# Block attention with routed experts on one core: the four expert slots of under 256 tokens, from fp32 matmuls to three products of split operands

## The chip, the cores and the metric

The kernel runs on one core of a Trainium2 chip. The metric is the device time of one execution in microseconds (us); of before there are three runs. PE is TensorE, DVE VectorE, ACT ScalarE, POOL GpSimd, and SP is the engine that issues most transfers. A profile's span runs from the first to the last instruction of one profiled execution.

## The reference

Two parts are computed. First, attention over 8 batches, 8 heads, 576 positions of 64 values, masked by blocks of 64 positions:

```python
mask = block_i >= block_j
scores = np.where(mask, scale * np.matmul(q, k.transpose(0, 1, 3, 2)), -1e9)
attn = softmax(scores)
x = np.matmul(attn, v)        # as 4608 tokens of 512 values
```

Then each token picks a group and, in it, an expert (16 experts in all, by two argmaxes), and goes through that expert's two layers:

```python
h = np.maximum(xg[mask_e] @ w1[g, e], 0.0)    # 512 -> 1024
ye = h @ w2[g, e]                             # 1024 -> 512
out[tok_idx] = combined[:, None] * ye
```

All inputs and the output are fp32.

## The kernel before

The kernel has an attention stage, and behind it an expert stage, which is the one that the change touches. Attention of 32 pairs of heads is laid out by a list of steps, with the routing of finished batches woven in. In the routing, tokens are counted by expert, and a table of token numbers is written to DRAM.

**Slots.** The expert stage works through slots. A slot is one expert with a fixed room for `T` tokens. One early slot, "e", has 512. Then come 14 slots in the order of `EXEC` (line 423), with `T = 16 * CAPS`: 528, 144, 448, 144, 448, 192, 416, 256, 320, 256, 320, 288, 272 and 128. Four of them have under 256 tokens: 144, 144, 192 and 128. Before the change they carry `small=True` (line 866).

**Weights.** Each expert's weights are eight units of 512 KB: units 0, 2, 4 and 6 are column blocks of w1, units 1, 3, 5 and 7 are row blocks of w2. A unit is loaded by SP into one of four `raw` buffers (`load`, line 915). Then two pieces of 512 columns are made of it (`piece`, line 922). ACT casts the piece to the type fp32r, as the high part `wh` (line 936), and DVE subtracts that from the fp32 piece and writes the remainder as the low part `wl` (line 937). A small slot's w1 units are handled otherwise: SP loads them straight into a `wh` buffer as fp32 (line 928), with no cast and no `wl`. There are 9 buffers each for `wh` and `wl`.

**Tokens.** `xt` (line 943) transposes gathered rows on PE into PSUM (line 953). ACT copies the high part `xh` out (line 960), and DVE makes the low part `xl` (line 961). For a small slot ACT makes one fp32 copy (line 958), and there is no `xl`.

**The first layer,** `g1` (line 963), writes `h`. For each block of 128 hidden values and each of four parts of 128 inputs it does three fp32r matmuls, wh·xh, wh·xl and wl·xh (line 985). For a small slot it does one fp32 matmul in their place (line 980). Such a matmul has as many moving columns as the slot has tokens (half as many where that is 528). Each of them has its own weight load, which the profile lists apart, as PEld. Slots of 256 tokens or fewer handle several hidden blocks in one call: two blocks for 144, 192 and 256, four blocks for 128. So a slot of 144 or 192 tokens has four calls of g1, and the slot of 128 has two.

**The second layer,** `g2` (line 1016), multiplies split `h` by split w2 with 512 moving columns (lines 1030 and 1035). It is the same for all slots.

**Order.** PE's order is a fixed list, `seq` (line 1062): a g1 call, then the g2 call of the call of g1 before it. Behind each of these steps, `run` lets `advance` (line 1120) issue up to two pieces, by due times that `plan` works out from an assumed time on PE (line 1086): four passes over the columns for a small slot's g1, three for others. `pump` (line 1112) keeps up to four units in raw buffers ahead of the unit that is being split.

Of the kernel before, what the change touches and what calls it, by code (L numbers as in the profile page):

```python
# [17 lines left out]
P = 128  # L18
# [815 lines left out]
class Moe:  # L834
# [25 lines left out]
    def slot(self, n, m, row, idx):  # L860
        T = UNIT * m
        nf, r = divmod(T, P)
        ch = [(c, P) for c in range(nf)] + ([(nf, r)] if r else [])
        nk = 1 if T > 256 else min(8, 1 << (512 // T).bit_length() - 1)
        return dict(n=n, m=m, T=T, gap=32 if r <= 32 else 64, nf=nf + (r > 64), tail=r if r <= 64 else 0, ch=ch, row=row, idx=idx, u={}, x={},
                    small=T < 256, nk=nk, nb=8 // nk)

    def index(self, s):
        if "e" in s:
# [39 lines left out]
            src, n = self.w2[bass.ds(s["e"], 1), z:z + 256, :], 2  # L909
        return src.rearrange("o (c p) f -> p (o c) f", p=P), n  # L910

    def direct(self, s, u):
        return s["small"] and u % 2 == 0

    def load(self, s, u):
        self.index(s)
        raw = self.raw.tile([P, 1024], F32, tag="raw", name=f"raw{s['n']}_{u}")
# [3 lines left out]

    def piece(self, s, u, z):
        nc = self.nc
        if self.direct(s, u):
            self.index(s)
            h = self.wh.tile([P, 1024], F32R, tag="wh", name=f"wh{s['n']}_{u}")
            src, n = self.wsrc(s, u)
            nc.sync.dma_start(h.bitcast(F32).rearrange("p (c f) -> p c f", c=n), src)
            s["u"][u] = (h,)
            return  # L930
        if z == 0:
            s["u"][u] = (self.wh.tile([P, 1024], F32R, tag="wh", name=f"wh{s['n']}_{u}"),
                         self.wl.tile([P, 1024], F32R, tag="wl", name=f"wl{s['n']}_{u}"))
        h, l = s["u"][u]
        sl = slice(z * 512, (z + 1) * 512)
        nc.scalar.copy(h[:, sl], s["raw", u][:, sl])  # L936
        nc.vector.tensor_tensor(out=l[:, sl], in0=s["raw", u][:, sl], in1=h[:, sl].bitcast(F32), op=ALU.subtract)  # L937
# [5 lines left out]
    def xt(self, s, c):  # L943
        nc = self.nc
        if "xt" not in s:
            s["xt"] = self.at.pt.tile([P, PTB], F32R, tag="pt", name=f"xt{s['n']}")
            s["xh"], s["xl"] = [s["xt"][:, PTB // 2 * z:PTB // 2 * z + 4 * s["T"]].rearrange("p (d w) -> p d w", d=4)
                                for z in range(2)]
        c, n = s["ch"][c]
        ps = self.at.psT(f"xp{s['n']}_{c}")  # L950
        pv = ps[:, 0:4 * n].rearrange("p (d w) -> p d w", d=4)
        for dc in range(4):
            nc.tensor.transpose(out=pv[:, dc, :], in_=s["x"][c][0:n, dc * P:(dc + 1) * P],  # L953
                                identity=self.c["ident"][0:n, 0:n])
        xh = s["xh"][:, :, c * P:c * P + n]
        xl = s["xl"][:, :, c * P:c * P + n]
        if s["small"]:
            nc.scalar.copy(xh.bitcast(F32), pv)
            return
        nc.scalar.copy(xh, pv)  # L960
        nc.vector.tensor_tensor(out=xl, in0=pv, in1=xh.bitcast(F32), op=ALU.subtract)

    def g1(self, s, b):
        nc = self.nc
        nk, T, r = s["nk"], s["T"], s["tail"]
        n = nk * T
        w0 = n if n <= 512 else n // 2
        ps = []
        for a in range(0, n, w0):
            p = self.at.ps_s.tile([P, 1, 512], F32, tag="S", name=f"h{s['n']}_{b}_{a}")[:, 0, 0:w0]  # L970
            ps.append((a, p))
            tw = min(T, w0)
            for k in range(w0 // tw):
                kg = b * nk + k
                w = self.w(s, 2 * (kg // 2))
                f = slice(kg % 2 * P, kg % 2 * P + P)
                o, t = p[:, k * tw:(k + 1) * tw], slice(a, a + tw)
                for dc in range(4):
                    if s["small"]:
                        nc.tensor.matmul(o, lhsT=w[0][:, dc, f].bitcast(F32), rhs=s["xh"][:, dc, t].bitcast(F32),  # L980
                                         start=dc == 0, stop=dc == 3)
                        continue
                    wh, wl = w
                    for x, (ww, rr) in enumerate(((wh, s["xh"]), (wh, s["xl"]), (wl, s["xh"]))):
                        nc.tensor.matmul(o, lhsT=ww[:, dc, f], rhs=rr[:, dc, t],  # L985
                                         start=dc == 0 and x == 0, stop=dc == 3 and x == 2)
        buf = self.hbuf()
        F = T - r
        pad = s["gap"] - r if r else 0
        L = T + pad  # L990
        g = buf[:, 0:nk * (L + T)].rearrange("p (k t) -> p k t", k=nk)
        hi, lt, lf = g[:, :, 0:T], g[:, :, L:L + r], g[:, :, L + r:L + T]
        if pad:
            nc.gpsimd.memset(g[:, :, T:L].bitcast(F32), 0.0)
        for a, p in ps:
            wa = min(T, w0)
            pv = p.rearrange("p (k t) -> p k t", t=wa)
            nc.scalar.activation(hi[:, :, a:a + wa], pv, AF.Relu)  # L998
            for t, t0, t1 in ((lf, 0, F), (lt, F, T)):
                q0, q1 = max(a, t0), min(a + wa, t1)  # L1000
                if q0 < q1:
                    nc.vector.scalar_tensor_tensor(out=t[:, :, q0 - t0:q1 - t0], in0=pv[:, :, q0 - a:q1 - a], scalar=0.0,  # L1002
                                                   in1=hi[:, :, q0:q1].bitcast(F32), op0=ALU.max, op1=ALU.subtract)
        s["h", b] = (hi, lf, g[:, :, F:L + r])
# [56 lines left out]
    def plan(self, slots):  # L1061
        self.slots = slots
        seq = []
        prev = None
        for o, s in enumerate(slots):
            s["o"] = o
            s["wide"] = o % 2 == 0
            for b in range(s["nb"]):
                seq.append((s, "g1", b))
                if b == 0:  # L1070
                    if prev is not None:
                        seq.append(prev)
                else:
                    seq.append((s, "g2", b - 1))
            prev = (s, "g2", s["nb"] - 1)
        seq.append(prev)
        self.seq = seq
        self.units = [(s, u) for s in slots for u in range(8)]
        self.first, self.last = {}, {}
        self.tc0, t = [], 0.0  # L1080
        self.begin = {}
        for n, (s, f, b) in enumerate(seq):
            self.tc0.append(t)
            nk = s["nk"]
            if f == "g1":
                t += nk * 4 * s["T"] * (4 if s["small"] else 3) / 2.4
            else:
                t += nk * (3 * s["nf"] + 2 * (s["tail"] > 0)) * 216
            if (f, b) == ("g1", 0):
                self.begin[s["o"]] = n  # L1090
                t += 430.0 * len(s["ch"])
            for k in range(b * nk, (b + 1) * nk):
                key = (s["o"], 2 * (k // 2) + (f == "g2"))
                self.first.setdefault(key, n)
                self.last[key] = n
        self.tc0.append(t)
        self.pieces = []
        for ui, (s, u) in enumerate(self.units):
            for z in range(1 if self.direct(s, u) else 2):
                self.pieces.append((ui, s, u, z))  # L1100
        self.due = [0.0] * len(self.pieces)
        nxt = 1e18
        for p in range(len(self.pieces) - 1, -1, -1):
            ui, s, u, z = self.pieces[p]
            nxt = min(self.tc0[self.first[s["o"], u]] - LEAD, nxt - PIECE)
            self.due[p] = nxt
        self.lq = [(s, u) for s, u in self.units if not self.direct(s, u)]
        self.nload = self.ndone = self.pos = 0
        self.gq = [(s, c) for s in slots for c in range(len(s["ch"]))]
        self.ngat = self.nxt = 0  # L1110
# [9 lines left out]
    def advance(self, k, limit, ready=False):  # L1120
        while k > 0 and self.pos < len(self.pieces):
            ui, s, u, z = self.pieces[self.pos]
            if ui > limit or (s["o"] > 0 and not ready):
                return
            if not self.direct(s, u) and ("raw", u) not in s:
                self.pump(ready)
            self.piece(s, u, z)
            self.pos += 1
            k -= 1
            if z == 1:  # L1130
                self.ndone += 1
            self.pump(ready)
# [50 lines left out]
    def overflow(self, cnti, row):  # L1183
        nc = self.nc
        hi = nc.values_load(cnti[0:1, 0:1], min_val=0, max_val=R - 1)
        with self.tc.For_i(0, hi, 1) as iv:
# [1 line left out]
            s["wide"] = False  # L1188
            self.gather(s, 0)
            for u in range(8):  # L1190
                if not self.direct(s, u):
                    self.load(s, u)
                for z in range(1 if self.direct(s, u) else 2):
                    self.piece(s, u, z)
            self.xt(s, 0)
            for b in range(s["nb"]):
# [123 lines left out]
```

## Time and profile before

| | us |
|---|---|
| three runs, median (lowest to highest) | 886.28 (885.41 to 886.73) |
| the profiled execution | 885.69 |
| its span | 883.6 |
| its mean granted clock, as a share of full | 0.994 |

The profile has a page, with busy time by engine and the chain of work that ended last, and views of its trace: groups of instructions, waits, a timeline, and busy time by stretch. In the timeline, neighbouring instructions of one kind are merged into one row. Its second number runs from the start of the first to the end of the last. PE's matmuls overlap, so a row's length is the spacing of its matmuls plus the full length of the last one.

### The profile page before, as it was taken

The numbers are of one execution on the slowest core, as the hardware profiler recorded it, in microseconds if no ns is written. First come the engines' busy times: TensorE is split into PE (matmuls) and PEld (weight loads), VectorE is DVE, ScalarE is ACT, GpSimd is POOL, SyncE is SP. The second block draws the span as 40 slices with busy tenths as digits, with TensorE's granted clock in tenths as the row PEclk, the third lists the DMA queues.
The fourth block names the chain that finished last, engine by engine and source line by source line (L and its number), as shares of the span: only waits on it lengthen the run. The fifth ranks groups of instructions, "written<-read, shape, count | busy, mean of one in ns | idle before, by whom it ended". The sixth has DMA issues, their size and how long they took to land.

```text
span 883.6 us, 17134 instructions
## 1 busy us (share of the span) xinstructions
PE 851.7 (96%) x5649; PEld 712.1 (81%) x5649; DVE 571.7 (65%) x1390; ACT 523.2 (59%) x1374; POOL 245.4 (28%) x469
## 2 busy tenths in 40 slices
PE   6889999999999999998989999999999999999996
PEld 4767878888887878776768878888888888988885
DVE  6657888889897979867824254365354655556562
ACT  5878888888897978774324244243343544545451
POOL 6443231424232232432523122122112121122011
PEclk9999999999999999999999999999999999999999
DMA  6988987878887877663245473474565566565471
GB/s 134 213 206 204 229 190 174 192 162 186 175 188 163 185 176 173 142 204 122 61 163 157 138 239 122 144 232 143 162 207 167 162 218 220 188 199 194 155 241 38
DMA packets 194041, 153.91 MB, mean 174 GB/s; under 512 B 126854, under 2 KB 158086, under 8 KB 193952
## 3 DMA queue, kind: packets, MB, share of 16 engines
q1 hardware_dynamic: 184704, 128.17, 55.9%
q0 software_dynamic: 9248, 24.64, 7.9%
q8 instruction: 46, 0.75, 0.3%
q14 instruction: 43, 0.35, 0.1%
HBM read 100.88 MB, written 24.59 MB: 142 GB/s over the span
## 4 chain that ended last, share of the span: by engine, by line
PE 88%; DMA 6%; DVE 3%; issue 2%; ACT 1%; SPq 0%; POOLq 0%; POOL 0%; DVEq 0%; ACTq 0%
PE y L1030 18%; PE h L985 18%; PE o L329 10%; PE tp L297 10%; PE s L254 9%; PE y L1035 4%; PE h L980 3%; DMA qk<-qk 3%; PE tp L176 3%; PE s L263 3%; PE xn L681 2%; PE xp L953 2%; PE lg L699 2%; PE ye L1030 2%; PE he L985 1%
## 5 line engine op out<-in xcount | busy, mean ns | idle before, releaser
L278 ACT ACTIVATE pb<-s,nm 128x384 f32<-128x384 f32 (+4 forms) x288 | 158.2, 560 | 28.3 <-DVE nm L268 25.3
L268 DVE TENSOR_REDUCE nm<-s 128x1 f32<-128x384 f32 (+4 forms) x288 | 141.4, 516 | 42.2 <-PE s L254 35.1
L985 PE MATMUL h<-xt,wh 128*128 128x264 f32 (+6 forms) x704 | 155.3, 312 | 0.0
L254 PE MATMUL s<-qk 128*128 128x384 f32 (+3 forms) x512 | 129.5, 351 | 11.9 <-DMA qk<-qk 5.5
L937 DVE TENSOR_TENSOR wl<-raw,wh 128x512 fp32r<-128x512 f32 x192 | 123.4, 684 | 10.6 <-ACT wh L936 10.3
L985 PEld LDWEIGHTS h<-xt,wh 128*128 128x128 f32 x704 | 119.3, 188 | 9.0
L309 ACT COPY pt<-tp 128x512 f32<-128x512 f32 (+1 forms) x224 | 113.2, 552 | 8.4 <-PE tp L297 5.4
L297 PE MATMUL tp<-ident,pb 128*128 128x128 f32 x800 | 117.2, 275 | 0.1
L985 PE MATMUL h<-xt,wl 128*128 128x264 f32 (+6 forms) x352 | 109.3, 311 | 0.0
L936 ACT CAST wh<-raw 128x512 fp32r<-128x512 f32 x192 | 109.1, 620 | 0.2
L1030 PE MATMUL y<-wh,hring 128*128 128x512 f32 x306 | 107.2, 401 | 0.0
L297 PEld LDWEIGHTS tp<-ident,pb 128*128 128x128 f32 x800 | 93.0, 141 | 13.6 <-DVE tmp L719 3.4
L329 PE MATMUL o<-pt,vb 128*64 128x320 f32 (+4 forms) x896 | 100.4, 362 | 2.3 <-ACT xT L309 1.3
L1002 DVE SCALAR_TENSOR_TENSOR hring<-h,hring 128x32 fp32r<-128x32 f32 (+7 forms) x112 | 35.7, 356 | 103.4 <-ACT hring L998 96.5
L998 ACT ACTIVATE hring<-h 128x288 fp32r<-128x288 f32 (+7 forms) x62 | 28.9, 467 | 118.3 <-PE h L985 53.7
L329 PEld LDWEIGHTS o<-pt,vb 128*64 128x64 f32 x896 | 60.0, 136 | 42.4 <-issue 3.5
L254 PEld LDWEIGHTS s<-qk 128*128 128x128 f32 x512 | 78.7, 190 | 19.2 <-ACT pb L278 9.9
L1056 POOL DMA_INDIRECT out_dram<-ys,ids x40 | 42.2, 1054 | 186.9 <-DVE ys L1052 157.3
L900 POOL DMA_INDIRECT xg<-xd,ids x40 | 41.7, 1043 | 103.7 <-DMA ids<-tab 48.7
L985 PEld LDWEIGHTS h<-xt,wl 128*128 128x128 f32 x352 | 66.2, 188 | 1.2
L1030 PEld LDWEIGHTS y<-wh,hring 128*128 128x128 f32 x306 | 57.6, 188 | 11.7
L1030 PE MATMUL y<-wl,hring 128*128 128x512 f32 x153 | 60.5, 395 | 0.0
(228 smaller groups left out, 1391.4 us busy)
## 6 DMA issues: line engine op xcount, KB each, us to landing
raw<-in_moe_w_dram SPq DMA_DIRECT2D x96, 512.0 KB
qk<-qk SPq DMA_DIRECT2D x93, 288.0 KB
natk<-in_k_dram SPq DMA_DIRECT2D x32, 256.0 KB
natq<-in_q_dram SPq DMA_DIRECT2D x32, 256.0 KB
vb<-in_v_dram SPq DMA_DIRECT2D x64, 128.0 KB
xd<-xns SPq DMA_DIRECT2D x32, 256.0 KB
wh<-in_moe_w_dram SPq DMA_DIRECT2D x16, 512.0 KB
tab<-fill POOLq DMA_DIRECT2D x10, 512.0 KB
```

What stands on the lines that cost most here:

```text
L254: nc.tensor.matmul(st[:, 0, 0:w], lhsT=r[a][z][:, q0:q0 + P], rhs=r[c][z][:, 0:w], start=x == 0, stop=x == 1)
L268: self.nc.vector.tensor_reduce(out=r["nm"][:, t:t + 1], in_=r["s", t], op=ALU.max, axis=AX.X if t < 8 else AX.XY, negate=True)
L278: nc.scalar.activation(reg, r.pop(("s", t)), AF.Exp, bias=r["nm"][:, t:t + 1], accum_out=self.sms[b][:, pr, t % 2, t // 2:t // 2 + 1])
L297: nc.tensor.transpose(out=o, in_=pb[:, POFF[x] + j * P:POFF[x] + (j + 1) * P], identity=self.c["ident"])
L309: self.nc.scalar.copy(dst, src)
L329: nc.tensor.matmul(o[64 * a:64 * a + 64, BLK * (t - b0):n], lhsT=r["v"][:, a, j, :], rhs=p[:, a], start=x == 0, stop=x == len(pcs) - 1, ti ...
L900: self.nc.gpsimd.indirect_dma_start(out=x[0:n], out_offset=None, in_=src, in_offset=bass.IndirectOffsetOnAxis(ap=s["ids"][0:n, c, 0:1], ax ...
L936: nc.scalar.copy(h[:, sl], s["raw", u][:, sl])
L937: nc.vector.tensor_tensor(out=l[:, sl], in0=s["raw", u][:, sl], in1=h[:, sl].bitcast(F32), op=ALU.subtract)
L985: nc.tensor.matmul(o, lhsT=ww[:, dc, f], rhs=rr[:, dc, t], start=dc == 0 and x == 0, stop=dc == 3 and x == 2)
L1030: nc.tensor.matmul(y[c][0:n], lhsT=hh, rhs=w, start=k == 0 and x == 0, stop=k == 7 and x == 2)
L1056: i = nc.gpsimd.indirect_dma_start(out=self.out, out_offset=bass.IndirectOffsetOnAxis(ap=s["ids"][0:n, c, 0:1], axis=0), in_=ys[0:n], in_o ...
```

## The change

The flag `small` goes, and with it each place that asked for it. The four small slots are treated as the others: their w1 units go through a raw buffer, the cast and the subtraction, their tokens get a low part, and g1 does three fp32r matmuls where it did one fp32 matmul. The planner counts three passes for them, and two pieces for each w1 unit where it counted one. The loop for overflowing tokens at the end, which has a slot of 128, changes likewise.

```diff
     def piece(self, s, u, z):
-        if self.direct(s, u):
-            self.index(s)
-            h = self.wh.tile([P, 1024], F32R, tag="wh", name=f"wh{s['n']}_{u}")
-            src, n = self.wsrc(s, u)
-            nc.sync.dma_start(h.bitcast(F32).rearrange("p (c f) -> p c f", c=n), src)
-            s["u"][u] = (h,)
-            return
...
         xl = s["xl"][:, :, c * P:c * P + n]
-        if s["small"]:
-            nc.scalar.copy(xh.bitcast(F32), pv)
-            return
         nc.scalar.copy(xh, pv)
         nc.vector.tensor_tensor(out=xl, in0=pv, in1=xh.bitcast(F32), op=ALU.subtract)
...
                 for dc in range(4):
-                    if s["small"]:
-                        nc.tensor.matmul(o, lhsT=w[0][:, dc, f].bitcast(F32), rhs=s["xh"][:, dc, t].bitcast(F32),
-                                         start=dc == 0, stop=dc == 3)
-                        continue
                     wh, wl = w
...
-                t += nk * 4 * s["T"] * (4 if s["small"] else 3) / 2.4
+                t += nk * 4 * s["T"] * 3 / 2.4
...
-            for z in range(1 if self.direct(s, u) else 2):
+            for z in range(2):
...
-        self.lq = [(s, u) for s, u in self.units if not self.direct(s, u)]
+        self.lq = list(self.units)
```

On PE, at the second g1 call of the first slot of 144 tokens (`h_1_0`; `y_4` and `y_0` are outputs of g2, `xt` holds the tokens), the order was:

```order
L1035 MATMUL y_4_6814<-wh_7_7071,hring 48x512
L1035 MATMUL y_4_6814<-wl_7_7072,hring 48x512
L980 MATMUL h_1_0_7281<-xt_7127,wh_2_7202 128x144 x8
L1030 MATMUL y_0_7300<-wh_1_7180,hring 128x512
L1030 MATMUL y_0_7300<-wl_1_7181,hring 128x512
```

and now begins as follows (the last two of these rows come eight times in all):

```order
L1013 MATMUL y_3_6813<-wh_7_7071,hring 128x512
L1018 MATMUL y_4_6814<-wh_7_7071,hring 48x512
L1018 MATMUL y_4_6814<-wl_7_7072,hring 48x512
L968 MATMUL h_1_0_7313<-xt_7133,wh_2_7196 128x144 x2
L968 MATMUL h_1_0_7313<-xt_7133,wl_2_7197 128x144
```

Eight matmuls in a call have become 24; their place among the others is the same.

On SP, where the loads of that slot's units stand (`raw_1` is unit 1 in a raw buffer, `wh_0` unit 0 loaded directly; the `raw` rows between two `wh` rows here are of the next slot), the order was:

```order
L919 DMA raw_7_7077<-in_moe_w_dram 128x2x512
L928 ISA
L928 DMA wh_0_7111<-in_moe_w_dram 128x4x256
L919 ISA
L919 DMA raw_0_7186<-in_moe_w_dram 128x4x256
L928 ISA
L928 DMA wh_2_7202<-in_moe_w_dram 128x4x256
L919 ISA
L919 DMA raw_1_7223<-in_moe_w_dram 128x2x512
```

and is now:

```order
L916 DMA raw_3_7077<-in_moe_w_dram 128x2x512
L916 ISA
L916 DMA raw_4_7117<-in_moe_w_dram 128x4x256
L916 ISA
L916 DMA raw_5_7194<-in_moe_w_dram 128x2x512
L916 ISA
L916 DMA raw_6_7216<-in_moe_w_dram 128x4x256
L916 ISA
L916 DMA raw_7_7253<-in_moe_w_dram 128x2x512
```

The eight units are loaded in the order in which PE uses them; before, unit 7 stood ahead of unit 0.

On ACT, in the slot of 272 tokens just ahead of the last slot (`hring` rows evacuate g1's output, `CAST` rows are pieces), the order was:

```order
L998 ACTIVATE hring<-h_3_0_10585 128x272
L936 CAST wh_6_10581<-raw_6_10456 128x512
L936 CAST wh_7_10614<-raw_7_10511 128x512
L998 ACTIVATE hring<-h_4_0_10618 128x272
L936 CAST wh_7_10614<-raw_7_10511 128x512
L936 CAST wh_1_10649<-raw_1_10536 128x512 x2
L998 ACTIVATE hx<-h_5_0_10655 128x272
```

and is now:

```order
L981 ACTIVATE hring<-h_3_0_10863 128x272
L926 CAST wh_7_10859<-raw_7_10781 128x512
L926 CAST wh_0_10884<-raw_0_10806 128x512 x2
L926 CAST wh_1_10900<-raw_1_10841 128x512
L981 ACTIVATE hring<-h_4_0_10904 128x272
L926 CAST wh_1_10900<-raw_1_10841 128x512
L926 CAST wh_2_10925<-raw_2_10857 128x512 x2
L926 CAST wh_3_10941<-raw_3_10882 128x512
L981 ACTIVATE hx<-h_5_0_10945 128x272
```

Between two evacuations there are now four casts, where there were two or three.

## Rows read from the trace of the kernel before

**Rows 1.** The page: busy us, share and instructions; the granted clock in 40 slices.
```profile
PE 851.7 (96%) x5649; PEld 712.1 (81%) x5649; DVE 571.7 (65%) x1390; ACT 523.2 (59%) x1374; POOL 245.4 (28%) x469
PEclk9999999999999999999999999999999999999999
```

**Rows 2.** Busy us by stretch, the expert stage: PE, PEld, DVE, ACT, POOL, clock, DMA share, GB/s.
```profile
500.00:876.00 376.00, 374.86 (x2097) 325.98 (x2095) 193.70 (x401) 161.73 (x315) 78.26 (x127) 1.00 0.57 181
```

**Rows 3.** PE's waits from 400 us on: us in total, times, longest.
```profile
PE xp L953 <- DMA xg<-xd,ids: 4.2, 1, 4.2
PE h L980 <- DMA wh<-in_moe_w_dram: 1.1, 1, 1.1
```

**Rows 4.** Chain of work that ended last, in order of time: start, us, what.
```profile
520.39 7.21 DMA wh<-in_moe_w_dram
...
573.60 1.96 PE h L980 x16
...
634.35 2.60 PE h L980 x16
...
695.87 2.86 PE h L985 x24
...
861.69 3.57 PE h L980 x32
```

**Rows 5.** Groups on PE from 500 us: shapes, count; busy us, mean ns of one.
```profile
L985 PE MATMUL h<-xt,wh 128*128 128x256 f32 x128 | 23.3, 282 | 0.0
...
L980 PE MATMUL h<-xt,wh 128*128 128x144 f32 x128 | 17.1, 287 | 1.1 <-DMA wh<-in_moe_w_dram 1.1
...
L980 PE MATMUL h<-xt,wh 128*128 128x192 f32 x64 | 11.2, 328 | 0.0
...
L980 PE MATMUL h<-xt,wh 128*128 128x128 f32 x64 | 7.5, 275 | 0.0
```

**Rows 6.** Timeline of weight loads (PEld): start, us, line, tile, shapes, count.
```profile
300.57 0.19 PEld L254 LDWEIGHTS s<-qk 128*128 128x128 f32 x1
350.98 0.30 PEld L254 LDWEIGHTS s<-qk 128*128 128x128 f32 x2
697.02 0.30 PEld L985 LDWEIGHTS h<-xt,wh 128*128 128x128 f32 x2
```

**Rows 7.** Timeline of PE, attention scores: two fp32r matmuls of 128 columns.
```profile
300.56 0.33 PE L254 MATMUL s<-qk 128*128 128x128 f32 x2
```

**Rows 8.** Timeline of weight loads and PE around another such pair.
```profile
304.08 0.30 PEld L254 LDWEIGHTS s<-qk 128*128 128x128 f32 x2
304.32 0.14 PEld L176 LDWEIGHTS tp<-ident,natq 128*128 128x128 f32 x1
...
304.10 0.42 PE L254 MATMUL s<-qk 128*128 128x128 f32 x2
304.36 0.41 PE L176 MATMUL tp<-ident,natq 128*128 128x128 f32 x2
```

**Rows 9.** Groups on ACT and DVE from 500 us: shapes, count; busy, mean ns.
```profile
L936 ACT CAST wh<-raw 128x512 fp32r<-128x512 f32 x176 | 100.0, 620 | 0.2
...
L937 DVE TENSOR_TENSOR wl<-raw,wh 128x512 fp32r<-128x512 f32 x176 | 113.1, 683 | 9.3 <-ACT wh L936 9.1
L961 DVE TENSOR_TENSOR xt<-xp,xt 128x512 fp32r<-128x512 f32 x21 | 14.4, 688 | 16.0 <-ACT xt L960 12.6 <-issue 3.2
```

**Rows 10.** Timeline of PE: starts of two g1 calls of the 272 slot.
```profile
844.26 0.41 PE L985 MATMUL h<-xt,wh 128*128 128x272 f32 x2
...
847.61 0.42 PE L985 MATMUL h<-xt,wh 128*128 128x272 f32 x2
```

**Rows 11.** Transfers from 500 us on: GB/s in 40 slices.
```profile
GB/s 161 203 332 72 169 187 171 123 289 141 159 140 181 114 253 276 83 240 110 179 109 248 175 233 244 189 183 228 101 291 179 121 236 182 136 204 232 176 55 30
```

More of the change, by code (lines that the diff above doesn't have):

```diff
@@ L865, in slot @@
         return dict(n=n, m=m, T=T, gap=32 if r <= 32 else 64, nf=nf + (r > 64), tail=r if r <= 64 else 0, ch=ch, row=row, idx=idx, u={}, x={},
-                    small=T < 256, nk=nk, nb=8 // nk)
+                    nk=nk, nb=8 // nk)
     def index(self, s):
@@ L910, in wsrc @@
         return src.rearrange("o (c p) f -> p (o c) f", p=P), n
-    def direct(self, s, u):
-        return s["small"] and u % 2 == 0
     def load(self, s, u):
@@ L1124, in advance @@
                 return
-            if not self.direct(s, u) and ("raw", u) not in s:
+            if ("raw", u) not in s:
                 self.pump(ready)
@@ L1190, in overflow @@
             for u in range(8):
-                if not self.direct(s, u):
-                    self.load(s, u)
-                for z in range(1 if self.direct(s, u) else 2):
+                self.load(s, u)
+                for z in range(2):
                     self.piece(s, u, z)
```

## The prediction

> **What bounds the kernel now.** I read the page first: PE is busy for 851.7 of 883.6 us, at the full granted clock in every slice [rows 1]. The change lies in the expert stage alone, so that stage comes next. From 500 to 876 us PE is busy for 374.86 of 376 us, DVE for 193.7, ACT for 161.7 and the transfers for 0.57 of their time [rows 2]. In such a stage a microsecond added on PE is a microsecond of the kernel, and ACT and DVE have room. PE's waits confirm it: past 500 us it waited once, 1.1 us, for a transfer into `wh`, the direct load of a small slot [rows 3]. That load took 7.21 us from issue to landing [rows 4]. The question is therefore what three fp32r matmuls take on PE where one fp32 matmul stood. A matmul's listed length does not tell it, since matmuls overlap; the spacing does.
>
> **What is removed.** A small slot has 8 hidden blocks times 4 input parts, 32 fp32 matmuls. The profile lists each as two records: 128 for the two slots of 144, 64 for that of 192 and 64 for that of 128 [rows 5], so each matmul goes through PE twice. The chain of work gives what the calls took, free of overlap [rows 4]: 1.96 us for 16 records of 144 columns, 2.60 us for 16 of 192 and 3.57 us for 32 of 128. That is 0.122, 0.162 and 0.112 us a record. With 8 calls of 144, 4 of 192 and 2 of 128, the calls take 8 × 1.96 + 4 × 2.60 + 2 × 3.57 = 33.2 us. The direct loads go too, and with them the 1.1 us wait.
>
> **What is added on PE.** Three fp32r matmuls for each fp32 one are 3 × 32 × 4 = 384 records in place of 256. What is one worth, at 128 to 192 columns? The expert stage has no fp32r matmul below 256 columns. There the call of 24 takes 2.86 us [rows 4], 0.119 each. This is the bound from above: fewer columns should not cost more.
>
> The bound from below is the weight load, as each matmul has its own. Two loads of 128 weight columns merged in a row last 0.30 us, where one lasts 0.19, so the second starts 0.11 us after the first, for attention's fp32r scores as for w1 [rows 6]. Across these rows that spacing does not shrink, neither for 256 columns nor for 128 [rows 8]. With rounding, it is at least 0.105 us. A matmul of 128 columns does not stream that long: in a pair of fp32r matmuls in the scores, the second starts 0.05 to 0.06 us after the first (0.33 us for both, less the 0.275 us that one of 128 lasts) [rows 5, 7]. So the stream gets short and the load stays: below 256 columns the load sets the pace, and columns that are saved give nothing back. The fp32 calls of 128 columns, whose load is of the same size, run at 0.112 us a record. This is the nearest row, and I take it, between 0.105 and 0.119.
>
> Per call, 24 × 0.112 = 2.68 us for 144 and 192 columns, and 48 × 0.112 = 5.36 us for 128. The differences are 0.72 × 8 = 5.8 us for the slots of 144, 0.08 × 4 = 0.3 us for that of 192, and 1.79 × 2 = 3.6 us for that of 128: together +9.7 us. The bounds: 384 × 0.105 − 33.2 = +7.1 us and 384 × 0.119 − 33.2 = +12.5 us. An fp32 matmul went through PE twice, each time for about two cycles a column (0.162 us × 2.4 GHz / 192); three fp32r passes at some 1.1 cycles a column (0.119 × 2.4 / 256) would be fewer cycles, but they need three weight loads instead of two, and that is what these short slots pay for.
>
> **What is added elsewhere.** 16 units of w1 are now split, in 32 pieces: 32 × 0.62 = 19.8 us on ACT and 32 × 0.683 = 21.9 us on DVE, and seven subtractions for `xl`, up to 0.688 us each, on DVE [rows 9]. This lies beside PE's work, since ACT goes from 161.7 to some 182 and DVE from 193.7 to some 220 of 376 us. I cost it at nothing. Its cover is thinnest in the slot of 272 tokens. There a g1 call starts every 3.35 us [rows 10], and each period now has four pieces: 4 × 0.62 = 2.5 us on ACT and 4 × 0.683 = 2.7 us on DVE, besides the evacuation. It also takes two units of 0.52 MB off the raw buffers, 313 GB/s, where the busiest slice of before moved 332 [rows 11]. If the loads fall behind, a cast waits on ACT, the evacuation of `h` queued behind it waits too, and then g2 on PE.
>
> The bytes that are loaded stay the same. The queue of SP now issues units in the order of use; the one load that PE waited for goes through a raw buffer ahead of its need. I take the whole 1.1 us back (bounds 0 and 1.1). The planner's shorter assumed time moves due times and nothing on PE, whose order is fixed; its price is nothing, or part of the late loads below.
>
> **Sum.** 885.69 us is the profiled execution's own time. +9.7 for the calls and −1.1 for the wait give +8.6 us, 894.3. The median of the runs lies 0.59 us higher, so I predict 894.9 us for it, 1.0% slower. With the bounds: 886.28 + 7.1 − 1.1 = 892.3 to 886.28 + 12.5 = 898.8.
>
> **The rivals.**
>
> *Loads hidden, faster.* The pair in [rows 7] could be the steady pace: the second matmul starts while its weights are still being loaded. Then columns set the pace, 0.06 us at 128. On the line from there to 0.119 at 256 it is about 0.067 at 144 and 0.09 at 192. 192 × 0.067 + 96 × 0.09 + 96 × 0.06 = 27.3 us, so −5.9 − 1.1 = −7.0 us, 879.3. It decides from a spacing of (33.2 + 1.1) / 384 = 0.089 us down. For it speaks only that pair of starts. Against it: the next load begins 0.24 us after the first of the pair [rows 8], so the third matmul cannot follow at that pace. 4%.
>
> *Loads half hidden, no change.* If loads overlapped each other in a long run, a spacing halfway between the 0.06 and 0.11 us, about 0.085 us, would give 384 × 0.085 = 32.6 us, −0.6 − 1.1 = −1.7 us: 884.6, 0.19% below. No row shows two fp32r loads of 128 weight columns closer than 0.11 us. 4%. The Trainium skill's page "TensorE: Matmul & The Clock Gate" (section "Back-to-back issue gap") says that in a stream of pairs of weight load and matmul the spacing is about 81 ns at 128 columns; by that figure this rival would hold. No row here shows such a spacing for fp32r.
>
> *Short streams dearer.* fp32r might lose its single pass below some width and cost as many cycles a column as an fp32 record: 192 × 0.122 + 96 × 0.162 + 96 × 0.112 = 49.7 us, +16.5 − 1.1, 901.7 us. Against it is the same pair, whose first matmul is done with its 128 columns within 0.06 us [rows 7], and that the transpose behind such a pair starts 0.26 us after the pair's first [rows 8]. 5%.
>
> *The feed falls behind.* The late cast described above, in the 272 slot or in the slots of 144, adds 2 to 6 us to the forecast: 897 to 901. For it speaks the load of 7.21 us at 520 us [rows 4]: in a slot of 144 two units go by every 5 us or so. Against it, four units are kept ahead, and longer calls on PE give each load more time. 10%.
>
> **How the numbers follow.** The forecast has 77%, hidden loads 4%, half-hidden loads 4%, dearer streams 5%, the late feed 10%. The predicted time is the forecast's, 894.9. The range, 890.5 to 900.5, takes in the bounds of the spacing, most of the late feed, and 2 us below for a gain in order that I have not seen. A measurement of this kernel can tell about 0.2% from no change. Slower by more than that: the forecast, dearer streams and the late feed, 92%, less 2% for some gain that I have missed, 0.90. Within 0.2%: half-hidden loads and 1% of that, 0.05. Faster: hidden loads and the other 1%, 0.05.
>
> **What would show it.** In the profile after, a g1 call of 24 matmuls of 144 columns takes 2.6 to 2.8 us in the chain, and one of 192 columns the same. Equal lengths for 128, 144 and 192 columns a matmul show that the load sets the pace; lengths that grow with the columns show that it does not. PE's waits from 500 us on hold no transfer into `wh`. A wait of PE for `hring` or `wh` near 850 us shows the late feed. The forecast fails if the spacing at 144 columns is under 0.1 us or over 0.12.

## The result, and the profile after

The changed kernel takes 894.64 us (median of four runs, 892.92 to 897.38), where the kernel before took 886.50 beside it (median of four runs, too): a ratio of 1.0093 [1.0071, 1.0116]. It is slower by 0.7 to 1.2%, as forecast. A second set of five runs of the same kernel, which belongs to the experiments, gave 892.97 us, 1.0078 [1.0050, 1.0105]. The forecast of 894.9 lies 0.3 us from the first median and 1.9 us from the second.

Most of that scatter is not the change's. The expert stage began (first g1 call of the slot of 528) at 458.2 to 463.8 us in the profiles of this study, whichever kernel ran, while the same stretch of the expert stage, at the full granted clock, repeats within some 0.1 us from profile to profile. What follows is therefore read by stretches of the expert stage, and the medians serve as the check.

The page of the kernel after, the lines that answer to [rows 1]: busy us, share and instructions, then the granted clock in 40 slices.

```profile
PE 865.4 (97%) x5777; PEld 726.8 (81%) x5777; DVE 595.2 (66%) x1429; ACT 542.6 (61%) x1406; POOL 244.6 (27%) x469
PEclk8999999999999999999999999999999999999988
```

PE has 128 more matmuls, 5777 for 5649, which is the 384 less the 256 of the sum. DVE is busy for 23.5 us more and ACT for 19.4 us more. The last two slices of the clock show 8 where before showed 9; more on that below. (The first slice shows 8 too; it lies in the attention stage, which the change does not touch.)

The g1 calls of the small slots in the chain of work that ended last, against [rows 4] (start, us, what):

```profile
573.58 2.63 PE h L968 x24
...
637.13 2.66 PE h L968 x24
...
698.69 2.85 PE h L968 x24
...
865.19 7.85 PE h L968 x47
```

The first row is a call of 144 columns, 2.63 us for 1.96 before. The second is 192 columns, 2.66 for 2.60, and the third is a call of 256 that the change does not touch, 2.85 for 2.86. So 144 and 192 columns now cost the same. The last row, the first call of the 128 slot, does not fit: 7.85 us where 5.36 was forecast.

PE's waits from 400 us on (us in total, times, longest), against [rows 3]:

```profile
...
PE h L968 <- DVE xt L948: 0.7, 1, 0.7
```

The wait for a load into `wh` is gone, as the forecast said. A new one stands in its place: 0.7 us for the low part of the tokens, which DVE makes at L948.

Why that last call is so long is in the windows around it (stretch; then its length, PE, PEld, DVE, ACT, POOL busy us and counts, granted clock, DMA share, GB/s):

```profile
500.00:876.00 376.00, 375.32 (x2142) 327.61 (x2142) 213.62 (x437) 176.22 (x343) 74.49 (x120) 0.99 0.57 178
...
864.00:866.00 2.00, 1.32 (x10) 1.00 (x9) 1.14 (x4) 0.09 (x1) 0.00 (x0) 1.00 0.00 0
866.00:868.00 2.00, 2.00 (x20) 2.00 (x19) 0.00 (x0) 0.00 (x0) 0.00 (x0) 0.98 0.00 0
868.00:870.00 2.00, 2.00 (x11) 2.00 (x11) 0.00 (x0) 0.00 (x0) 0.00 (x0) 0.50 0.04 8
...
876.00:878.00 2.00, 2.00 (x11) 1.90 (x9) 0.54 (x2) 1.37 (x2) 1.08 (x2) 0.50 0.00 0
```

The first row answers to [rows 2]: PE is as full as before, with DVE and ACT higher. In the last slot of this execution the granted clock fell to 0.50, which is 1.2 GHz, from 868 to 878 us. PE's timeline shows what that does to one pattern of three matmuls (start, us, what):

```profile
865.47 0.39 PE L968 MATMUL h<-xt,wh 128*128 128x128 f32 x2
865.69 0.28 PE L968 MATMUL h<-xt,wl 128*128 128x128 f32 x1
865.80 0.38 PE L968 MATMUL h<-xt,wh 128*128 128x128 f32 x2
...
868.36 0.63 PE L968 MATMUL h<-xt,wh 128*128 128x128 f32 x2
868.79 0.41 PE L968 MATMUL h<-xt,wl 128*128 128x128 f32 x1
869.00 0.63 PE L968 MATMUL h<-xt,wh 128*128 128x128 f32 x2
```

Three matmuls take 865.80 − 865.47 = 0.33 us at the full clock and 869.00 − 868.36 = 0.64 us at half. Whether that is part of what the change costs, or an event of this one execution, was the first question for the experiments.

### The profile page after: what moved, and what is told of

The parts are those of the page before. It is cut to its first block, busy times and chain, and to the rows that moved or that the text cites. A ratio compares the mean times of both kernels' runs of the same rounds, so it can differ in the third digit from the quotient of the medians.

```text
span 895.6 us, 17468 instructions
## 1 busy us (share of the span) xinstructions
PE 865.4 (97%) x5777; PEld 726.8 (81%) x5777; DVE 595.2 (66%) x1429; ACT 542.6 (61%) x1406; POOL 244.6 (27%) x469
## 4 chain that ended last, share of the span: by engine, by line
PE 87%; DMA 6%; DVE 4%; issue 1%; ACT 0%; SPq 0%; POOL 0%; POOLq 0%; ACTq 0%; DVEq 0%
PE h L968 23%; PE y L1013 18%; PE o L329 9%; PE tp L297 9%; PE s L254 8%; PE y L1018 5%; DMA qk<-qk 3%; PE tp L176 3%; PE s L263 3%; PE xp L943 2%; PE lg L699 2%; PE xn L681 2%; PE ye L1013 2%; PE he L968 1%; DMA vb<-in_v_dram 1%
## 5 line engine op out<-in xcount | busy, mean ns | idle before, releaser
L968 PE MATMUL h<-xt,wh 128*128 128x264 f32 (+9 forms) x960 | 202.1, 305 | 0.7 <-DVE xt L948 0.7
L968 PEld LDWEIGHTS h<-xt,wh 128*128 128x128 f32 x960 | 161.4, 192 | 11.1 <-DVE xt L948 0.9
L927 DVE TENSOR_TENSOR wl<-raw,wh 128x512 fp32r<-128x512 f32 x224 | 143.6, 683 | 8.4 <-ACT wh L926 8.3
L968 PE MATMUL h<-xt,wl 128*128 128x264 f32 (+9 forms) x480 | 146.0, 304 | 0.0
L926 ACT CAST wh<-raw 128x512 fp32r<-128x512 f32 x224 | 127.2, 620 | 5.2 <-DMA raw<-in_moe_w_dram 2.9
L968 PEld LDWEIGHTS h<-xt,wl 128*128 128x128 f32 x480 | 92.3, 192 | 1.2
```

Source lines behind the costliest of these rows:

```text
L968: nc.tensor.matmul(o, lhsT=ww[:, dc, f], rhs=rr[:, dc, t], start=dc == 0 and x == 0, stop=dc == 3 and x == 2)
```

## The experiments

Six more kernels were run, and the changed one once more. This table holds what they gave. The stretches are between starts of g1 calls in each kernel's profile. **A** runs from the first call of the 528 slot to the first of the 448 slot behind it, with the first 144 slot in it. **B** runs on to the first call of the second 448 slot, with the second 144 slot. **C** runs on to the 416 slot, with the 192 slot. **D** runs on to the last call of the 272 slot, with no small slot. **E** runs on to the start of PE's last matmul, with the 128 slot. Times are in us.

| kernel | median | ratio to before | A | B | C | D | E | A to E |
|---|---|---|---|---|---|---|---|---|
| before | | 1 | 71.14 | 60.68 | 62.98 | 201.45 | 18.19 | 414.44 |
| after | 894.64 | 1.0093 [1.0071, 1.0116] | 72.54 | 63.59 | 63.00 | 201.40 | 27.47 | 428.00 |
| after, again | 892.97 | 1.0078 [1.0050, 1.0105] | 72.53 | 63.59 | 63.00 | 201.40 | 22.41 | 422.93 |
| 128 stays fp32 | 889.76 | 1.0036 [1.0021, 1.0052] | 72.54 | 63.58 | 63.01 | 201.37 | 18.19 | 418.69 |
| calls of two blocks | 893.53 | 1.0088 [1.0058, 1.0119] | 72.54 | 63.59 | 63.00 | 201.38 | 21.74 | 422.25 |
| tokens early | 893.47 | 1.0080 [1.0052, 1.0108] | 72.54 | 63.58 | 63.01 | 201.81 | 21.30 | 422.24 |
| half loads | 881.79 | 0.9934 [0.9916, 0.9953] | 68.99 | 60.10 | 61.27 | 201.38 | 17.64 | 409.38 |
| feed alone | 884.48 | 0.9986 [0.9965, 1.0006] | 69.73 | 60.68 | 62.73 | 201.40 | 18.19 | 412.73 |
| direct loads in order | 885.39 | 0.9976 [0.9959, 0.9993] | 69.73 | 60.68 | 62.74 | 201.36 | 18.20 | 412.71 |

The first four of the experiments and the last three were measured at two times, each set beside its own runs of before (886.08 and 887.40 us in the median). The stretches of before are those of the profiled execution of 885.69 us.

### The changed kernel once more

No edit; the same kernel, profiled a second time, to see whether the clock falls in the last slot again.

> The changed kernel once more, for a second profile and for the spread of its times. In the first profile the granted clock fell to half from 867.9 to 878.1 us, in the first call of the slot of 128 tokens. Theory 1: the fall belongs to that slot's long calls of short matmuls (48 in a row, each waiting for its weight load), and comes in every execution: the second profile shows half the clock within 10 us of the start of that slot, and the three times lie within 892 to 898 us. Rival: it came by chance in that execution, or from the 0.7 us in which PE waited for the tokens' low part; then the second profile has the full clock there whenever the wait is shorter, and the slot's calls take 5.4 us each.

It did not fall there: stretch E took 22.41 us where it had taken 27.47, and A to D agree within 0.01 us. PE's waits from 460 us on (us in total, times, longest):

```profile
PE h L968 <- DVE xt L948: 0.4, 1, 0.4
```

And the two calls of the 128 slot in its chain of work (start, us, what):

```profile
865.50 5.46 PE h L968 x47
...
872.86 5.31 PE h L968 x48
```

A call of the 128 slot takes 5.31 us at the full clock, for a forecast of 5.36. The theory that the low clock belongs to the last slot's work, and comes in every execution, falls; it cost the first profile 27.47 − 22.41 = 5.1 us and stands in this stretch of no other profile. The wait for `xl`, though, is there again.

Equal lengths at equal counts can be read from the groups of the same kernel (line, engine, operation, shapes, count, busy us, mean ns of one):

```profile
L968 PE MATMUL h<-xt,wh 128*128 128x144 f32 x128 | 21.8, 275 | 0.0
...
L968 PE MATMUL h<-xt,wh 128*128 128x192 f32 x64 | 11.0, 275 | 0.0
L968 PE MATMUL h<-xt,wh 128*128 128x128 f32 x64 | 10.9, 274 | 0.4 <-DVE xt L948 0.4
```

Twice as many matmuls of 144 columns are twice as busy as those of 192 and of 128: the columns make no difference. The median from one start to the next is 112 ns for 128, for 144 and for 192 columns, and 119 ns for 256.

### The slot of 128 stays with fp32

```diff
-                    small=T < 256, nk=nk, nb=8 // nk)
+                    small=T == 128, nk=nk, nb=8 // nk)
```

This is the kernel before, with the change for the slots of 144 and 192 alone.

> Undoes one part: the slot of 128 tokens keeps its fp32 matmuls and direct loads, the slots of 144, 144 and 192 change as in the changed kernel. By the sum, the calls of the three slots add 8 x (2.63 - 1.96) + 4 x (2.66 - 2.60) = 5.6 us and the wait for the direct load goes in the first slot of 144 (about 1.2 us): +4.4 us over before, about 890.9 us, ratio 1.005. Theory 1 for the clock: full clock until PE's last matmul, and the last slot's calls take 3.57 us. If the half clock came from anything else in the expert stage (the added splitting, the slots of 144), it shows here too, and the time is 2 to 5 us longer.

A to E is 418.69 − 414.44 = +4.25 us over before. Stretches A to C are those of the changed kernel and E is that of before, to 0.03 us: the parts of the change add up, and nothing passes from one slot to the next. In its chain the calls of the 128 slot show the fp32 price again (start, us, what):

```profile
867.21 3.57 PE h L980 x32
872.64 3.57 PE h L980 x32
```

### The 128 slot in calls of two blocks

```diff
-        nk = 1 if T > 256 else min(8, 1 << (512 // T).bit_length() - 1)
+        nk = 1 if T > 256 else 2
```

In the changed kernel, the 128 slot now has four calls of 24 matmuls in place of two of 48.

> The changed kernel with one size changed: the slot of 128 tokens handles two hidden blocks in a call of g1 where it handled four, so that it has four calls of 24 matmuls with a g2 step between them, as the slots of 144. The same matmuls in all. Theory 1 (a long run of short matmuls brings the clock down): the full clock lasts through the slot, each call takes 2.65 us, and the kernel is 3 to 5 us faster than the changed one: about 890.5 us, 1.004 of before. Rival (any such matmuls, or the wait for the tokens, bring it down): the clock falls again and the time is that of the changed kernel within 1 us.

Two of the four calls in its chain (start, us, what):

```profile
862.70 2.63 PE h L968 x24
...
867.23 2.63 PE h L968 x24
```

At 128 columns a call of 24 takes what it takes at 144 and 192, 2.63 us, and four of them are 10.52 us, two of 48 being 10.62. The wait for `xl` is gone, and E is 0.67 us shorter than in the second profile of the changed kernel. The total, 893.53 us, cannot be told from the other sets of it. The clock held, as it had with the longer calls in the second profile of the changed kernel; so the 3 to 5 us that theory 1 expected from shorter calls did not come, and nothing here ties the low clock to the length of a call.

### The last slot's tokens earlier

```diff
+            if o == len(self.slots) - 1:
+                at -= 4
             if o > 0:
```

The transposes of the 128 slot's tokens stand four steps earlier in the list of PE's steps; the rest is the changed kernel.

> The changed kernel, with the transposition and split of the last slot's tokens moved four steps forward, ahead of the last pieces of its weights on ACT and DVE. This takes away the 0.7 to 0.9 us in which PE waited for the tokens' low part at the start of that slot. Theory 1: the wait is worth its own 0.9 us and no more; the clock falls as before, within 5 us of the start of the slot, and the first call takes over 7 us. Rival (the wait is what lets the clock fall): the full clock through the slot, both calls at 5.4 us, and the kernel 5 to 6 us faster than the changed one.

The two calls of the 128 slot in its chain (start, us, what):

```profile
866.24 5.31 PE h L968 x48
...
873.46 5.31 PE h L968 x48
```

Both calls take 5.31 us with all 48 matmuls in one piece, so the second one no longer waits. A to E is 0.69 us shorter (the moved steps now lie ahead of the end of D, which is 0.41 longer for it). That prices the new wait: 0.7 us. It is too little to show in the median, 893.47 us. Theory 1 expected the clock to fall again, and it did not. As it held in this profile and in the second one of the changed kernel alike, with and without the wait, the wait is not shown to lower the clock; one profile of each kernel cannot rule it out either.

### Half of the weight columns

```diff
+                        first, end = dc == 0 and x == 0, dc == 3 and x == 2
+                        if T < 256 and not (first or end):
+                            fh = slice(kg % 2 * P, kg % 2 * P + 64)
+                            nc.tensor.matmul(o[0:64], lhsT=ww[:, dc, fh], rhs=rr[:, dc, t], start=False, stop=False)
+                            continue
```

In the changed kernel, 10 of the 12 matmuls of each hidden block in the small slots load 64 weight columns where they loaded 128, with the same moving columns. Half of the hidden values of those slots then lack ten of their twelve products. If the weight load sets the pace, the calls must get shorter; if the moving columns or a cost per matmul do, they must not.

> The changed kernel, where 10 of the 12 matmuls of each hidden block of a small slot load 64 of their 128 weight columns and write 64 of their 128 output rows; half of those products is left out, the moving columns and the number of matmuls stay. Theory 2 (the weight load sets the pace at 128 to 192 columns): with half a load, some 0.056 us, the stream of columns sets it, about 0.06, 0.067 and 0.09 us at 128, 144 and 192. A call of 144 takes 4 x 0.112 + 20 x 0.067 = 1.8 us in place of 2.65, one of 192 2.2 us, one of 128 8 x 0.112 + 40 x 0.06 = 3.3 us in place of 5.4, and from the first call of 528 to PE's last matmul it is about 14 us less than the changed kernel's 422.9. Rival (a fixed price of each short fp32r matmul, whatever it loads): the calls keep 2.65 and 5.4 us.

Its timeline in a call of 144 columns, first weight loads (PEld), then matmuls (start, us, what):

```profile
513.68 0.20 PEld L971 LDWEIGHTS h<-xt,wh 128*64 128x64 f32 x2
513.81 0.13 PEld L971 LDWEIGHTS h<-xt,wl 128*64 128x64 f32 x1
513.88 0.20 PEld L971 LDWEIGHTS h<-xt,wh 128*64 128x64 f32 x2
...
513.74 0.30 PE L971 MATMUL h<-xt,wh 128*64 128x144 f32 x2
513.88 0.23 PE L971 MATMUL h<-xt,wl 128*64 128x144 f32 x1
513.94 0.30 PE L971 MATMUL h<-xt,wh 128*64 128x144 f32 x2
```

Three loads of one pattern start within 513.88 − 513.68 = 0.20 us. In the timeline of the kernel after, the same three take 510.28 − 509.94 = 0.34 us:

```profile
509.94 0.30 PEld L968 LDWEIGHTS h<-xt,wh 128*128 128x128 f32 x2
510.17 0.19 PEld L968 LDWEIGHTS h<-xt,wl 128*128 128x128 f32 x1
510.28 0.30 PEld L968 LDWEIGHTS h<-xt,wh 128*128 128x128 f32 x2
```

The chain of the kernel with half loads shows the same, in a call of 144 columns (start, us, what):

```profile
518.79 0.67 PE h L971 x10
519.46 0.22 PE h L973 x2
519.68 0.67 PE h L971 x10
```

Ten matmuls with 64 weight columns take 0.67 us, and two with 128 take 0.22, by the same moving columns. The median from start to start is 60, 67 and 89 ns at 128, 144 and 192 columns, against 112 ns at all three in the changed kernel. The edit also halves the output rows that each matmul writes, but those did not set the pace: in [rows 7] the second of two matmuls with 128 output rows each starts 0.05 to 0.06 us after the first. So the weight load of 128 columns set the pace. With it halved, the spacing grows with the columns, at 1.1 cycles each (0.060 × 2.4 GHz / 128, and the same at 192). That is the pace per column of the rows at 256. A to E falls by 422.24 − 409.38 = 12.9 us against the kernel with the tokens early, which like this one waits nowhere; 320 shorter spacings come to 160 × 0.045 + 80 × 0.023 + 80 × 0.052 = 13.2 us. With 881.79 us, 0.7% faster than before, this is about the time that the rival of hidden loads gave (879.3): without the load's floor the change would have been a gain.

### The feed alone

```diff
+                    if T < 256:
+                        nc.tensor.matmul(o, lhsT=wh[:, dc, f].bitcast(F32), rhs=s["xh"][:, dc, t].bitcast(F32),
+                                         start=dc == 0, stop=dc == 3)
+                        continue
```

The changed kernel with its loads, its casts and its subtractions, but on PE the fp32 matmul of before, which reads the high parts alone. The products with low parts are left out in the small slots.

> The feed of the changed kernel alone: all units of the small slots go through raw buffers, the cast and the subtraction, tokens get both parts, but g1 of a small slot does one fp32 matmul on the high parts, as many as before; the products with low parts are left out there. Prediction's step: the added work on ACT and DVE costs nothing and the wait for the direct load goes. Calls at 1.96, 2.60 and 3.57 us, no wait of PE for weights, and 1.2 us less than before from the first call of 528 to PE's last matmul (413.2 us against 414.4). The short calls leave the feed less time than in the changed kernel. Rival (the feed falls behind): PE waits for weights or h in the small slots, 1 us or more in all, and the stretch is as long as before or longer.

Calls of 144, 192 and 128 columns in its chain (start, us, what):

```profile
512.31 1.96 PE h L968 x16
...
633.85 2.60 PE h L968 x16
...
866.32 3.57 PE h L968 x32
```

The calls have the lengths of before, PE waits for nothing from 460 us on, and A to E is 412.73 us, 1.71 below before. The feed that the change adds costs nothing that can be seen here, and its order of loads gives 1.7 us. As PE reads no low part in this kernel, a late `wl` or `xl` could not show in it; for those the changed kernel's own waits stand, which name `xl` once and `wl` never. Of the 1.7 us, 1.41 lie in stretch A and 0.25 in C. The trace of before names both, in the waits of the weight loads (PEld, from 500 us on: us in total, times, longest):

```profile
PEld h L980 <- DMA wh<-in_moe_w_dram: 1.6, 2, 1.4
```

The longer one, 1.4 us, is in the first 144 slot; the other, 0.2 us, is in the 192 slot.

### Direct loads in order

```diff
+            while self.pos < len(self.pieces):
+                ui, s, u, z = self.pieces[self.pos]
+                if not self.direct(s, u) or ui > limit or (s["o"] > 0 and not ready):
+                    break
+                self.piece(s, u, z)
+                self.pos += 1
+                k -= 1
             self.pump(ready)
```

The kernel before, with fp32 calls and direct loads; a direct load that is next in the order of use is issued ahead of the raw loads for later units.

> The kernel before with one edit to the order of its queue: a direct load of a small slot's w1 unit is issued ahead of the raw load of a later unit, which stood in front of it and waited for its buffer. fp32 matmuls as before. Theory: the load that PE waited for lands earlier, the 1.1 us wait goes, and the stretch from the first call of 528 to PE's last matmul takes about 413.2 us against 414.4; the kernel is 0.1% faster than before, less than its runs scatter. Rival (the direct load waits for a free wh buffer, not for the raw load): the wait stays and nothing changes.

A to E is 412.71 us, in every stretch the same as the feed alone to 0.04 us, though this kernel has none of the added casts and subtractions. PE's wait for `wh` is gone. So the 1.7 us come from the order of the loads alone, and the 32 added pieces cost 0.02 us where PE reads only their high parts. With 885.39 us, 0.9976 [0.9959, 0.9993], this is the one version with all its products that is faster than the kernel before, by 0.1 to 0.4%, and so than the changed one.

## Why the prediction was right

**The bound and the mechanism.** It said that a microsecond on PE in this stage is one of the kernel, and that the short matmuls would go at the pace of their weight loads. Both were shown. With half the weight columns the spacing fell to that of the moving columns, and the stage got shorter by what the spacings gave. The equal spacings at 128, 144 and 192 columns are the sign that was asked for. One reading was loose: a 9 in the clock row of [rows 1] is 90% or more, not the full clock. Just ahead of the expert stage the trace of before has a stretch at 0.50 (the columns are those of the windows above):

```profile
450.00:452.00 2.00, 2.00 (x6) 1.61 (x6) 1.14 (x2) 1.62 (x3) 0.14 (x2) 0.50 0.11 38
```

The sum does not rest on it, since the expert stage of before ran at 1.00 [rows 2].

**The nearest row.** The choice of 0.112 us, from the fp32 calls of 128 columns with a load of the same size, between 0.105 and 0.119, was right to the digit: the runs gave 112 ns. It would have been 119 by the row of 256 columns. The Trainium skill's page "TensorE: Matmul & The Clock Gate" gives 81 ns for a pair of load and matmul at 128 columns (section "Back-to-back issue gap"); no run here shows it with 128 weight columns, and the rival that rested on such a spacing fell. By that figure the sum would have been 384 × 0.081 − 33.2 − 1.1 = −3.2 us, an estimate: 0.4% faster, and not the "no change" of the rival beside which the prediction put it. The same page's section "LDWEIGHTS (loading the stationary operand)" gives a weight load its columns divided by 1.2, in ns, which is 107 ns for 128 columns. The measured spacing of 112 ns lies 5 ns above that.

**The terms.** They can be read off the stretches, as the second profile of the changed kernel less the feed alone, which has the same loads and order:

| term | forecast, us | measured, us |
|---|---|---|
| calls of the two 144 slots | +5.8 | +2.80 (A) + 2.91 (B) = +5.71 |
| calls of the 192 slot | +0.3 | +0.27 (C) |
| calls of the 128 slot | +3.6 | +4.22 (E) less the wait of 0.67 = +3.55 |
| wait for the direct load | −1.1 | −1.73 (direct loads in order less before) |
| casts and subtractions added | 0 | 0.02 (feed alone less direct loads in order) |
| wait for `xl` in the last slot | 0 | +0.67 (E) |
| sum | +8.6 | +8.49 |

**What was mis-sized.** Two small terms, which cancel: that the sum came out within 0.1 us is luck to that extent. The order of the loads gave 1.7 us for 1.1, since the forecast read the waits of PE's matmuls alone. The weight loads had waited 1.4 us in the first 144 slot, where the matmul's row says 1.1, and 0.2 us in the 192 slot, of which the matmul's rows say nothing. And the seven subtractions for `xl` were costed at nothing as a group: six of them are, the seventh is not. The step that failed is "this lies beside PE's work". That step had its thinnest cover at the 272 slot, from late casts, and looked for it in the weights. The place, the end of the 272 slot, was right; what came late was the tokens. The timeline of the second profile shows it:

```profile
863.14 1.29 DVE L927 TENSOR_TENSOR wl<-raw,wh 128x512 fp32r<-128x512 f32 x2 [0.65 <-PE xp L943]
...
863.53 0.39 ACT L981 ACTIVATE hring<-h 128x272 fp32r<-128x272 f32 x1
...
863.82 0.58 ACT L947 CAST xt<-xp 128x512 fp32r<-128x512 f32 x1
...
864.35 0.49 DVE L985 SCALAR_TENSOR_TENSOR hring<-h,hring 128x256 fp32r<-128x256 f32 x2
...
864.76 0.68 DVE L948 TENSOR_TENSOR xt<-xp,xt 128x512 fp32r<-128x512 f32 x1
864.83 0.22 PE L968 MATMUL h<-xt,wh 128*128 128x128 f32 x1
865.49 0.19 PEld L968 LDWEIGHTS h<-xt,wh 128*128 128x128 f32 x1 [0.70 <-DVE xt L948]
865.50 0.33 PE L968 MATMUL h<-xt,wh 128*128 128x128 f32 x1 [0.45 <-DVE xt L948]
```

ACT's copy of the tokens stands behind an evacuation of `h`. DVE's subtraction stands behind that of the evacuation, which stands behind two pieces of weights, and its 0.68 us had just begun when PE came to the slot's first call. The first matmul needs `xh` alone and runs; the second needs `xl`. Before, one fp32 copy on ACT was all that this slot's tokens asked for. Setting the transposes earlier takes the wait away.

**The rivals.** Hidden and half-hidden loads needed spacings of 60 to 90 ns; the runs gave 112 at every width. Dearer short streams would have made 192 columns dearer than 144; they cost the same. The late feed, 10%, came in another form: 0.7 us where 2 to 6 were priced, and for tokens, not weights.

**What stays open.** The half clock in the last slot of the first profile, 5.1 us, had a place in no term of the sum and in no rival. It is not a part of what the change does on PE, by the second profile and by those of the two kernels with the tokens early and with calls of two blocks, but what brought it in that one execution was not found. That the 897.38 us of this execution is the longest of the nine runs of the changed kernel fits it. The unprofiled runs do not show where their time lies.

## What to carry to other kernels

Ahead of trading fewer passes for more matmuls, count weight loads, not cycles: from 128 to 192 moving columns an fp32r matmul with a load of 128 weight columns cost 112 ns here whatever its columns, so three of them lost to an fp32 matmul, which had two loads, at 128 and at 144 columns, and were about level at 192. A work item that is "beside" the critical engine should be looked at once where its stage starts, with what stands ahead of it in its queues: six of the seven added `xl` subtractions were free, and the seventh cost 0.7 us. And where an early part of a kernel scatters by microseconds from run to run, compare stretches between the same two instructions: here, at the full granted clock, they repeated within 0.1 us and settled terms that the medians could not.

## What the runs showed of the hardware that was not expected

- With 64 weight columns in the place of 128, fp32r matmuls of 128 moving columns followed each other at 60 ns in a long run, at the pace of their columns. So the load of 64 fits into at most 60 ns, and no further cost per matmul shows.
- The granted clock can fall to half for 10 us inside a stretch in which PE is busy for all of its time: 868 to 878 us of one profile, 0.7 us of waiting some 3 us before it. The same stretch of the same kernel, with a wait of 0.4 us, ran at 1.00 in another profile.
- Loads that are issued in the order of use gained 1.7 us, with no change in their bytes. The waits of PE's matmuls named 1.1 us of it, those of the weight loads 1.6: where loads of weights come late, both rows are to be read.
